# Attention with a memory and a two-layer MLP in one kernel: order of the first tokens' work, one product moved from GpSimd to VectorE, a third unit in float32, a second buffer for v

## The chip, the cores and the metric

The kernel runs on one core of one Trainium2 chip. The metric is the device time of one execution in microseconds (us), lower is better. Three runs of the kernel before gave 588.53, 588.90 and 590.05 us; their median is 588.9 us.

## The reference

Inputs are q, k and v of shape (4, 8, 576, 64), a memory `M_prev` of one 64x64 matrix per batch and head, a vector `z_prev` per batch and head, one `beta` per head, and two weight matrices: `w_in` (512x2048) and `w_out` (2048x512). With B = 4 batches, H = 8 heads, S = 576 tokens and D = 64:

```
local = softmax(causal(q k^T / 8)) v
q_p   = phi(q)                      (phi(x) = elu(x) + 1)
mem   = (q_p M_prev) / (q_p z_prev + 1e-6)
x     = g * mem + (1 - g) * local   (g = sigmoid(beta), per head)
out   = relu(x_tokens w_in)^2 w_out
```

`x_tokens` puts the eight heads of a token side by side (512 columns); there are 2304 tokens. Results are float32, and the kernel keeps nearly float32 exactness: most operands of TensorE are split into a high part in a faster format and the rest as a low part, and a product is then three products (high by high, low by high, high by low).

## The kernel before

**First tokens.** The first 64 tokens of each batch need only one 64x64 block of scores. `first_tokens` (L224 to L326) computes them for all batches and heads in two halves of two batches: loads, `scores(g)` on TensorE, `phi(g)` and `softmax(g)` on ScalarE, VectorE and GpSimd, `outputs(g)` with transposes, copies and products that end in `xh` (L318) and `xl` (L319), the split input of MLP block 0. The string `SEQ` (L55) gives the order in which the loads are issued on the SP queue: `a`, `b`, `c` are three parts of the first tokens' data of half 0 or 1, `g` the gates, `r` the raw data of one weight unit, `l` the loads of the first attention unit. The table `TE` (L65) says for five of their operations (`me`, `ze`, `se`, `xe`, `ye`, used at L272, L274, L279, L288, L294) whether VectorE (`d`) or GpSimd (`p`) does them, for half 0 and half 1.

**Weights.** The two matrices come in 32 units of 128 rows (512 KB each). `load_weight` (L170) issues the load, `split_weight` (L156) cuts a unit into a high and a low part with three VectorE operations (L162, L164, L168) and two ScalarE ones (L163, L167).

**Attention.** The remaining 512 tokens of each batch are worked off in 24 units of one batch, one pair of heads, and two or four tiles of 128 tokens. Units 0 to 3 are tiles 1 and 2 of batch 0, units 4 to 7 its tiles 3 and 4. Of units 0 to `NES` - 1 = 5 the scores are plain float32 products, of later ones three split products. Of units 0 and 1 (`NEF` = 2, `full`) also the product of the weights e with v is in float32: e is transposed on TensorE (L519), copied by ScalarE (L524) and multiplied with v as loaded (L563). From unit 2 on, v is scaled and split (L398 to L419), e is split into a 16-bit `a` (L542, L544), transposed by a DMA (L548) and multiplied in 16-bit pieces (L569 to L574), then summed (L576) into `s3`. `loads` (L332) issues the loads `kd`, `qm`, `vv` of the next unit on the SP queue as soon as the memory part of the current unit is in the program; `vv` has `VVB` = 1 buffer. A finished pair of tiles is stored to a scratch tensor `xd` (L595).

**MLP.** `moe(n)` (L695) takes 256 tokens: block 0 is the first tokens, blocks 1 to 6 follow, the last two blocks go together in `moe_pair`. The input of block n + 1 is read back from `xd` and transposed at step j = 6 of block n (`prefetch`, L609). A block has eight steps: 24 products `up` (L719 to L721), then on ScalarE the relu and square (L725, L726) and the rounded `gh` (L728; VectorE at L730 from block 4 on), on GpSimd `gl = r - gh` (L731), then 12 products `oacc` (L709 to L711), one step behind. `gh` has `GHB` = 3 buffers, `gl` `GLB` = 2, `r` one.

**Order.** All instructions of one engine run in a fixed order, in one queue per engine. A planner sets that order at compile time: it works off the program with estimated durations and gives every engine, among the instructions that are ready by its estimate, the one that comes first in the program. Hence attention, which stands ahead of the MLP blocks 1 to 8 in the program, goes first, and the MLP fills TensorE. The program mixes block 0, the weights and units 0 to 3 (`ORD`, L79). Instructions in a `tc.high_priority()` block come first whatever their place.

Of the kernel before, what the change touches and what calls it, by code (L numbers as in the profile page):

```python
# [8 lines left out]
F32 = mybir.dt.float32  # L9
# [5 lines left out]
ALU = mybir.AluOpType  # L15
AX = mybir.AxisListType

B, H, S, D = 4, 8, 576, 64
# [3 lines left out]
P = 128  # L22
# [4 lines left out]
QT = [(0, 64), (64, 128), (192, 128), (320, 128), (448, 128)]  # L27
NQ = len(QT)
SQ = S - D
GHB = 3  # L30
GLB = 2
PAIR = 0
SC = 16384.0
# [2 lines left out]
PM = 'pd'  # L36
FX = 'dd'
GHN = 4
VMIN = 2.0**-80
NEF = 2  # L40
NES = 6
PXT = 'up'
PXE = 'aa'
PHI = 1
QB = 2
VVB = 1
ZW = D + 1
MW = 576
WSC = 1.0 / 256.0
# [2 lines left out]
KB = 1  # L52
XB = 2
PJ = 6
SEQ = 'a0 b0 g a1 r b1 r c0 l r r c1'  # L55
W0 = 9
EARLY = 'dp'
LATE = 'dd'
# [3 lines left out]
SGROUP = {2: [[(2, 0, 320), (1, 0, 192)]], 1: [], 3: [[(3, 0, 448), (4, 0, 64)]], 4: [[(4, 64, 576)]]}  # L62
STG = [(9, 'hlx'), (8, 'hlx'), (3, 'hlx'), (0, 'hlx')]
XF = 0
TE = ['dd', 'dp', 'pp', 'pp', 'pp']  # L65
TC = 'aa'
TW = 2 * NP * 6 * D
GB = 2
# [21 lines left out]
def fused_kernel(ctx: ExitStack, tc: tile.TileContext, t0_d, zt_d, kk_d, qv_d, beta, w_in, w_out, out):  # L90
    nc = tc.nc
# [3 lines left out]
    at = ctx.enter_context(tc.tile_pool(name="at", bufs=1))  # L95
# [13 lines left out]
        out=mask, in_=mask, pattern=[[-1, MW]], compare_op=ALU.is_ge, fill=-1e30, base=448, channel_multiplier=1  # L109
# [114 lines left out]
    def first_tokens(tp, ahead):  # L224
# [4 lines left out]
        ng = B // GB  # L229
# [5 lines left out]
        for step in SEQ.split():  # L235
# [6 lines left out]
            else:  # L242
                g = int(step[1])
# [14 lines left out]
        def scores(g):  # L258
            sp[g] = sp0[:, g]
            qd = tr[g][:, : 2 * GD].rearrange("p (r i d) -> p i r d", r=2, i=GN)  # L260
            for i in range(GN):
                for h in range(2):
                    hd = slice(h * D, (h + 1) * D)
                    nc.tensor.matmul(sp[g][hd, i], qd[hd, i, 0], qd[hd, i, 1], start=True, stop=True)
# [54 lines left out]
            nc.vector.tensor_tensor(out=lo, in0=xb, in1=hi.bitcast(F32), op=ALU.subtract)  # L319

        sp0 = ps.tile([P, ng, GN, D], F32, tag="s", name="sp0")
        for g in range(ng):
            scores(g)
            phi(g)
        for g in range(ng):
            softmax(g)  # L326
            outputs(g)

    dp = ctx.enter_context(tc.tile_pool(name="dp", bufs=1, space=bass.MemoryType.DRAM))
    xd = [dp.tile([S, DM], F32, name=f"xd{b}") for b in range(B)]  # L330
# [14 lines left out]
    def attention(b, p, tiles, ld, after, early, sfull, full):  # L345
# [13 lines left out]
        if not sfull:  # L359
# [4 lines left out]
                out=ql[:, qa:qb], in0=q_raw[:, qa:qb], in1=qh[:, qa:qb].bitcast(F32), op=ALU.subtract  # L364
# [60 lines left out]
        for grp in (tiles[:2], tiles[2:]):  # L425
            ng = len(grp)
# [3 lines left out]
            for j, i in enumerate(grp):  # L430
# [13 lines left out]
                in0=pv[:, :, :, :D],  # L444
# [50 lines left out]
        for i in [t for t in TORD if t in tiles]:  # L495
            q0, n = QT[i]
# [60 lines left out]
            if full:  # L557
                s3 = acc[:, :, 0]
                for h in range(2):
                    hd = slice(h * D, (h + 1) * D)  # L560
                    for c in range(nb):
                        kp = D if c == 0 else P
                        nc.tensor.matmul(  # L563
                            acc[:n, h, 0], aT[:kp, h * nb + c, :n], v[:kp, c, hd], start=c == 0, stop=c == i
                        )
            else:
                for h in range(2):
                    o2 = acc[:n, h].rearrange("p j d -> p (j d)")
                    nc.tensor.matmul(o2, aT[:, h * nb, :n], vs[:, h, 0], start=True, stop=i == 0)  # L569
                    for c in range(1, i + 1):  # L570
                        nc.tensor.matmul(  # L571
                            acc[:n, h, 0], aT[:, h * nb + i + c, :n], vs[:, h, c, :D], start=False, stop=False
                        )
                        nc.tensor.matmul(o2, aT[:, h * nb + c, :n], vs[:, h, c], start=False, stop=c == i)  # L574
                s3 = at.tile([P, 2, D], F32, tag="s3", name="s3", bufs=2)
                nc.vector.reduce_sum(out=s3[:n], in_=acc[:n].rearrange("p h j d -> p h d j"), axis=AX.X)  # L576
            if FX[late] == "p" and not full:
                xo = memx[:n, i - 1].rearrange("p (h d) -> p h d", h=2)
# [116 lines left out]
    def moe(n):  # L695
        b, blk = blocks[n]
        xh, xl = xq.pop()
        pend = []
        acc = []

        def down(j, gh, gl):
            if j == 0:
                for t in range(2):
                    acc.append(ps.tile([P, DM], F32, tag="acc", name="oacc", bufs=2))
            last = j == NF // 2 - 1
            for u, t in [(u, t) for t in range(2) for u in range(2)] if last else [(u, t) for u in range(2) for t in range(2)]:
                f = 2 * j + u
                ts = slice(t * P, (t + 1) * P)
                nc.tensor.matmul(acc[t], gh[:, u, ts], w_out_op(f, 0), start=f == 0, stop=False)  # L709
                nc.tensor.matmul(acc[t], gh[:, u, ts], w_out_op(f, 1), start=False, stop=False)  # L710
                nc.tensor.matmul(acc[t], gl[:, u, ts], w_out_op(f, 0), start=False, stop=f == NF - 1)  # L711

        for j in range(NF // 2):
            need(1 + 8 * (j // 2 + 1))
            up = ps.tile([P, 2, BLK], F32, tag="up", name="up", bufs=2)
            for u in range(2):
                f = 2 * j + u
                for k in range(NK):
                    nc.tensor.matmul(up[:, u, :], w_in_op(f, k, 0), xh[:, k, :], start=k == 0, stop=False)  # L719
                    nc.tensor.matmul(up[:, u, :], w_in_op(f, k, 0), xl[:, k, :], start=False, stop=False)  # L720
                    nc.tensor.matmul(up[:, u, :], w_in_op(f, k, 1), xh[:, k, :], start=False, stop=k == NK - 1)  # L721
            r = mo.tile([P, 2, BLK], F32, tag="r", name="r", bufs=RB)
            gh = mo.tile([P, 2, BLK], F32R, tag="gh", name="gh", bufs=GHB)
            gl = mo.tile([P, 2, BLK], F32R, tag="gl", name="gl", bufs=GLB)
            nc.scalar.activation(r, up, AF.Relu, scale=WSC)  # L725
            nc.scalar.activation(r, r, AF.Square)  # L726
            if n < GHN:
                nc.scalar.copy(gh, r)  # L728
            else:
                nc.vector.tensor_copy(gh, r)  # L730
            nc.gpsimd.tensor_tensor(out=gl, in0=r, in1=gh.bitcast(F32), op=ALU.subtract)  # L731
            pend.append((j, gh, gl))
            yield
            if n == NBLK - 3 and j in (3, PJ):
                if j == 3:
                    xq.append(pair_tiles())
                pair_prefetch(xq[-1], int(j == PJ))
                yield
            elif j == PJ and n + 1 < NBLK:
                assert n > 0 or last  # L740
                xq.append(prefetch(*blocks[n + 1], *last))
                last.clear()
                yield
            if len(pend) > 1:
                down(*pend.pop(0))
                yield
        for x in pend:
            down(*x)
            yield
        for t in range(2):  # L750
            o = mo.tile([P, DM], F32, tag="x", name="o", bufs=XB)
            nc.scalar.activation(o, acc[t], AF.Copy, scale=WSC)
            if b is None:
                for u in range(2):
                    r0 = (2 * t + u) * S
                    nc.sync.dma_start(out[r0 : r0 + D, :], o[u * D : (u + 1) * D])
            else:
                r0 = b * S + QT[1 + 2 * blk + t][0]
                nc.sync.dma_start(out[r0 : r0 + P, :], o)
        yield  # L760
# [116 lines left out]
```

## Time and profile before

| | |
|---|---|
| median of three runs | 588.9 us |
| the profiled execution's own time | 588.17 us |
| its span, first to last instruction | 586.4 us |
| mean granted TensorE clock | 0.984 |
| busy: TensorE matmul | 546.1 us (93%) |
| busy: VectorE (DVE) | 386.1 us (66%) |
| busy: ScalarE (ACT) | 348.5 us (59%) |
| busy: GpSimd (POOL) | 122.6 us (21%) |

The span is what the trace shows; 1.8 us of the execution lie around it. TensorE's busy time counts matmuls to a modelled end, and consecutive matmuls overlap, so a full TensorE is read from the distance between starts, not from the duration of one. In the views below PE is TensorE, SPq the queue that issues the DMAs, and a row of a timeline has start, duration, engine, line, operation, result and operands, and in brackets the idle time of the engine before it with what ended it.

### The profile page before, as it was taken

How to read it: one execution, taken by the hardware profiler on the slowest of the kernel's cores; microseconds unless marked ns; L12 is line 12 of the kernel's file. 1: busy time of each engine (PE TensorE's matmuls, PEld its weight loads, DVE VectorE, ACT ScalarE, POOL GpSimd, SP SyncE). 2: the span in 40 equal slices, each digit the busy share in tenths (PEclk: the TensorE clock that was granted, in tenths of full speed). 3: DMA queues.
4: the chain of work that ended last, by engine and by line, in shares of the span. 5: the costliest groups of instructions: out<-in, count | busy, mean ns of one | idle time of the engine just before them, and what ended most of it. 6: DMA issues, size and time to landing. Idle time of an engine off the chain costs nothing.

```text
span 586.4 us, 11178 instructions
## 1 busy us (share of the span) xinstructions
PE 546.1 (93%) x4006; PEld 471.0 (80%) x4006; DVE 386.1 (66%) x1289; ACT 348.5 (59%) x791; POOL 122.6 (21%) x99
## 2 busy tenths in 40 slices
PE   2468999799999999999999999999999999999996
PEld 2347887588888888888888788888888898888885
DVE  5999989877878687997696687967887211000000
ACT  3789876578867587897566674676656222312222
POOL 2502131124322011121120201111011212122221
PEclk9987999899999999999999999999999999999999
DMA  8967673757645667795553547555253300000001
GB/s 290 409 197 280 222 193 92 165 131 187 133 120 118 152 154 167 147 200 152 126 141 109 125 111 163 116 148 147 69 118 81 108 19 1 36 1 0 2 0 72
DMA packets 127574, 76.24 MB, mean 130 GB/s; under 512 B 99360, under 2 KB 112672, under 8 KB 127520
## 3 DMA queue, kind: packets, MB, share of 16 engines
q1 hardware_dynamic: 127520, 75.55, 48.8%
q8 instruction: 31, 0.51, 0.4%
q14 instruction: 23, 0.19, 0.1%
HBM read 42.63 MB, written 8.78 MB: 88 GB/s over the span
## 4 chain that ended last, share of the span: by engine, by line
PE 64%; DVE 17%; DMA 10%; issue 4%; ACT 3%; SPq 1%; POOL 1%; ACTq 0%; DVEq 0%; POOLq 0%
PE oacc L711 6%; PE oacc L709 6%; PE up L721 6%; PE up L719 6%; PE up L720 6%; PE oacc L710 6%; PE sp L465 5%; DMA aT<-a 4%; DVE w L168 3%; PE up L670 2%; PE up L669 2%; PE up L668 2%; PE acc L574 2%; DMA vv<-in_qv_dram 2%; PE pm L433 2%
## 5 line engine op out<-in xcount | busy, mean ns | idle before, releaser
L731 POOL TENSOR_TENSOR gl<-r,gh 128x512 fp32r<-128x512 f32 x56 | 77.3, 1380 | 332.4 <-ACT gh L728 118.1
L719 PE MATMUL up<-xh,w 128*128 128x256 f32 x448 | 130.1, 290 | 4.1 <-ACT aF L524 4.1
L720 PE MATMUL up<-xl,w 128*128 128x256 f32 x448 | 130.1, 291 | 0.0
L721 PE MATMUL up<-xh,w 128*128 128x256 f32 x448 | 130.0, 290 | 0.0
L504 ACT ACTIVATE e<-e,mx 128x320 f32<-128x320 f32 (+3 forms) x128 | 77.8, 610 | 83.1 <-DVE memx L584 43.0
L719 PEld LDWEIGHTS up<-xh,w 128*128 128x128 f32 x448 | 87.3, 195 | 8.0 <-ACT aF L524 4.5
L709 PE MATMUL oacc<-w,gh 128*128 128x512 f32 x224 | 90.1, 402 | 0.6 <-DVE gh L730 0.6
L720 PEld LDWEIGHTS up<-xl,w 128*128 128x128 f32 x448 | 87.4, 195 | 2.5 <-issue 0.8
L721 PEld LDWEIGHTS up<-xh,w 128*128 128x128 f32 x448 | 87.3, 195 | 2.3 <-issue 1.5
L710 PE MATMUL oacc<-w,gh 128*128 128x512 f32 x224 | 88.7, 396 | 0.0
L711 PE MATMUL oacc<-w,gl 128*128 128x512 f32 x224 | 86.8, 398 | 0.5 <-POOL gl L731 0.4
L544 DVE SCALAR_TENSOR_TENSOR a<-e,a 128x128 f16<-128x128 f32 x120 | 67.8, 583 | 28.2 <-ACT a L542 27.5
L542 ACT ACTIVATE a<-e 128x128 f16<-128x128 f32 x120 | 56.1, 519 | 8.8 <-DMA aT<-a 6.7
L676 DVE CAST gh<-r 128x512 fp32r<-128x512 f32 x16 | 6.9, 428 | 79.3 <-ACT r L675 79.3
L711 PEld LDWEIGHTS oacc<-w,gl 128*128 128x128 f32 x224 | 41.5, 188 | 10.3 <-POOL gl L731 1.8
L484 DVE CUSTOM_DVE_ANT_0 e<-sp,mask 128x320 f32<-128x320 f32 (+3 forms) x128 | 47.8, 418 | 1.4 <-PE sp L465 1.2
L725 ACT ACTIVATE r<-up 128x512 f32<-128x512 f32 x56 | 32.7, 583 | 26.5 <-PE up L721 23.2
L709 PEld LDWEIGHTS oacc<-w,gh 128*128 128x128 f32 x224 | 42.3, 189 | 7.5 <-DVE gh L730 0.8
L710 PEld LDWEIGHTS oacc<-w,gh 128*128 128x128 f32 x224 | 42.3, 189 | 7.4 <-issue 0.7
L674 ACT ACTIVATE r<-up 128x512 f32<-128x512 f32 x16 | 9.6, 599 | 61.8 <-PE up L670 61.8
L574 PE MATMUL acc<-vs,aT 128*128 128x128 f16 x308 | 36.7, 220 | 0.0
L571 PE MATMUL acc<-vs,aT 128*128 128x64 f16 x308 | 35.5, 193 | 0.0
(154 smaller groups left out, 1132.8 us busy)
## 6 DMA issues: line engine op xcount, KB each, us to landing
raw<-in_w_in_dram SPq DMA_DIRECT2D x11, 512.0 KB, 6.7
vv<-in_qv_dram SPq DMA_DIRECT2D x16, 320.0 KB, 3.2
raw<-in_w_out_dram SPq DMA_DIRECT2D x9, 512.0 KB, 7.1
kd<-in_kk_dram SPq DMA_DIRECT2D x16, 288.0 KB, 3.2
out_dram<-o SPq DMA_DIRECT2D x16, 256.0 KB, 2.2
xd<-memx SPq DMA_DIRECT2D x31, 128.0 KB, 2.1
xn<-xd SPq DMA_DIRECT2D x14, 256.0 KB, 2.9
qm<-in_qv_dram SPq DMA_DIRECT2D x8, 321.0 KB, 3.4
```

Source lines behind the costliest of these rows:

```text
L484: nc.vector.tensor_tensor_reduce(out=e[:, h, ka:kb], in0=sps[:, h, cs], in1=mask[:, 448 - q0 + ka : 448 - q0 + kb], scale=-0.125, scalar=3 ...
L504: ex = nc.scalar.activation(e[:n, h, :ke], e[:n, h, :ke], AF.Exp, bias=bs, scale=-1.0, accum_out=sm[:n, h : h + 1])
L542: nc.scalar.mul(av[:, :, o0 : o0 + w], x, SC)
L544: nc.vector.scalar_tensor_tensor(out=av[:, :, o0 + w : o0 + 2 * w], in0=x, scalar=SC, in1=av[:, :, o0 : o0 + w], op0=ALU.mult, op1=ALU.sub ...
L574: nc.tensor.matmul(o2, aT[:, h * nb + c, :n], vs[:, h, c], start=False, stop=c == i)
L709: nc.tensor.matmul(acc[t], gh[:, u, ts], w_out_op(f, 0), start=f == 0, stop=False)
L710: nc.tensor.matmul(acc[t], gh[:, u, ts], w_out_op(f, 1), start=False, stop=False)
L711: nc.tensor.matmul(acc[t], gl[:, u, ts], w_out_op(f, 0), start=False, stop=f == NF - 1)
L719: nc.tensor.matmul(up[:, u, :], w_in_op(f, k, 0), xh[:, k, :], start=k == 0, stop=False)
L720: nc.tensor.matmul(up[:, u, :], w_in_op(f, k, 0), xl[:, k, :], start=False, stop=False)
L721: nc.tensor.matmul(up[:, u, :], w_in_op(f, k, 1), xh[:, k, :], start=False, stop=k == NK - 1)
L731: nc.gpsimd.tensor_tensor(out=gl, in0=r, in1=gh.bitcast(F32), op=ALU.subtract)
```

## The change

It does six things. (1) `SEQ`: all loads of the first tokens come ahead of the first weight unit, and five weight units instead of four are loaded there, four of them behind the loads of the first attention unit. (2) The whole arithmetic of the first tokens stands in `tc.high_priority()`. (3) `TE`: seven products of the first tokens go from GpSimd to VectorE. (4) `GLV`: `gl` of MLP blocks 0 to 6 (56 instructions) is computed by VectorE; the last pair stays on GpSimd. (5) `NEF`: unit 2 too is done in float32 with v as loaded. (6) `vv` gets a second buffer; `gh` goes from three to two and `s3` from two to one.

```
-GHB = 3
+GHB = 2
+GLV = range(7)
-NEF = 2
+NEF = 3
-VVB = 1
+VVB = 2
-SEQ = 'a0 b0 g a1 r b1 r c0 l r r c1'
+SEQ = 'a0 b0 g a1 b1 c0 c1 r l r r r r'
-TE = ['dd', 'dp', 'pp', 'pp', 'pp']
+TE = ['dd', 'dd', 'dd', 'dd', 'dd']
...
-        for g in range(ng):
-            scores(g)
-            phi(g)
-        for g in range(ng):
-            softmax(g)
-            outputs(g)
+        with tc.high_priority():
+            for g in range(ng):
+                scores(g)
+                phi(g)
+            for g in range(ng):
+                softmax(g)
+                outputs(g)
...
-                s3 = at.tile([P, 2, D], F32, tag="s3", name="s3", bufs=2)
+                s3 = at.tile([P, 2, D], F32, tag="s3", name="s3", bufs=1)
...
-            nc.gpsimd.tensor_tensor(out=gl, in0=r, in1=gh.bitcast(F32), op=ALU.subtract)
+            (nc.vector if n in GLV else nc.gpsimd).tensor_tensor(out=gl, in0=r, in1=gh.bitcast(F32), op=ALU.subtract)
```

## Rows read from the trace of the kernel before

**Rows 1.** Busy time by stretch: start:end length, each engine (instructions), granted clock, DMA, GB/s.
```profile
0.00:15.00 15.00, 3.94 (x64) 3.57 (x64) 9.02 (x28) 5.07 (x8) 4.64 (x10) 1.00 0.90 293
15.00:30.00 15.00, 7.18 (x52) 5.43 (x52) 15.00 (x40) 10.54 (x23) 7.39 (x7) 1.00 1.00 398
...
45.00:60.00 15.00, 12.96 (x75) 11.81 (x75) 15.00 (x38) 14.38 (x35) 3.62 (x2) 0.77 0.64 245
60.00:90.00 30.00, 29.02 (x189) 25.48 (x188) 27.91 (x77) 25.08 (x63) 7.37 (x6) 1.00 0.69 203
90.00:120.00 30.00, 25.19 (x185) 19.91 (x186) 24.49 (x88) 16.13 (x34) 4.65 (x5) 0.94 0.55 133
120.00:450.00 330.00, 326.22 (x2682) 285.33 (x2682) 263.56 (x943) 228.62 (x537) 63.04 (x47) 1.00 0.57 134
```

**Rows 2.** Timeline of TensorE at the start of the MLP and around 110 us.
```profile
43.23 3.23 PE L563 MATMUL acc<-vv,aF 64*128 64x64 f32 x12
...
46.22 0.56 PE L720 MATMUL up<-xl,w 128*128 128x256 f32 x1
...
108.87 0.48 PE L621 MATMUL px<-identr,memx 128*128 128x128 f32 x2
112.59 1.32 PE L465 MATMUL sp<-kd,qm 64*128 64x512 f32 x4 [3.24 <-DVE mx L484]
```

**Rows 3.** Instructions on tile xh up to 120 us: shortest/median/longest ns, first and last start.
```profile
L319 DVE TENSOR_TENSOR xl<-xp,xh x2: 655/667/679, 33.6 to 41.7; 128x512 fp32r<-128x512 f32 x2
```

**Rows 4.** VectorE by line and shape, 0 to 130 us: count, busy us, mean ns, idle before.
```profile
L168 DVE TENSOR_TENSOR w<-hw,w 128x512 fp32r<-128x512 f32 x8 | 6.8, 856 | 0.0
...
L576 DVE TENSOR_REDUCE s<-acc 128x128 f32<-128x256 f32 x6 | 2.2, 415 | 0.0
...
L544 DVE SCALAR_TENSOR_TENSOR a<-e,a 128x512 f16<-128x512 f32 x2 | 1.4, 680 | 0.0
...
L274 DVE TENSOR_TENSOR tr<-tr,w 128x512 f32<-128x512 f32 x1 | 0.7, 672 | 0.0
```

**Rows 5.** Timeline of all engines around 25 us.
```profile
24.89 0.15 DVE L549 SCALAR_TENSOR_TENSOR sm<-sm,gpm 128x2 f32<-128x2 f32 x1
...
25.11 1.16 POOL L294 TENSOR_TENSOR w<-w,t 128x512 f32<-128x512 f32 x1 [1.44 <-DVE sm L549]
25.30 1.00 DVE L549 SCALAR_TENSOR_TENSOR sm<-sm,gpm 128x2 f32<-128x2 f32 x1
```

**Rows 6.** The chain of waits between 60 and 120 us: start, length, what.
```profile
82.95 4.90 DMA hw<-in_w_out_dram
...
101.34 3.60 DMA vv<-in_qv_dram
```

**Rows 7.** Waits over the whole span: who waited for whom, total us, times, longest.
```profile
POOL gl L731 <- ACT gh L728: 118.1, 19, 10.0
...
DVE vx L398 <- DMA vv<-in_qv_dram: 17.3, 11, 3.3
```

**Rows 8.** Waits of the SP queue over the whole span, same columns.
```profile
SPq L342 <- DVE vs L415: 49.6, 18, 7.4
```

**Rows 9.** Timeline of TensorE from the last product of a step to the next.
```profile
64.45 0.39 PE L711 MATMUL oacc<-w,gl 128*128 128x512 f32 x1
64.68 0.28 PE L719 MATMUL up<-xh,w 128*128 128x256 f32 x1
64.79 0.28 PE L720 MATMUL up<-xl,w 128*128 128x256 f32 x1
```

**Rows 10.** Instructions on tile gl, whole span: shortest/median/longest ns, first and last start.
```profile
L731 POOL TENSOR_TENSOR gl<-r,gh x56: 1262/1294/2040, 57.1 to 492.1; 128x512 fp32r<-128x512 f32 x56
```

**Rows 11.** Timelines of SP, VectorE and TensorE at the border to MLP block 5.
```profile
356.67 0.38 SPq L595 DMA_DIRECT2D xd<-memx  x1
...
373.91 0.68 DVE L625 TENSOR_TENSOR xl<-px,xh 128x512 fp32r<-128x512 f32 x1
...
376.06 0.39 PE L719 MATMUL up<-xh,w 128*128 128x256 f32 x1
```

## The prediction

> **What bounds the kernel now.** I read busy time by stretch first [rows 1]. From 120 to 450 us TensorE is busy 326.2 of 330 us, so a change there helps only if it keeps TensorE full. Up to 60 us it is the other way round: VectorE is busy 15.0 of 15 us from 15 us on, while TensorE has 7.2 of 15 us and then 13.0 of 15 at a granted clock of 0.77, a mixture of its levels 2.4 and 1.2 GHz. From 90 to 120 us neither is full (25.2 and 24.5 of 30). The time to win lies ahead of 120 us.
>
> The timeline of TensorE says what it lacked. MLP block 0 needs `xl` of both halves; the second `xl` starts at 41.7 us and takes 0.67 [rows 3], and the second kind of product starts at 46.2, behind 3.2 us of attention [rows 2]. At 108.9 us the last input of block 1 (unit 3's tiles) is transposed, and then TensorE stands for 3.2 us behind a score's maximum [rows 2]. In the chain of waits between, VectorE's work alternates with DMAs that came late: 4.9 us for a weight unit at 83 us, 3.6 us for `vv` at 101 us [rows 6]. SP is one reason: its `vv` load waited 49.6 us in all for the previous unit to finish with v, up to 7.4 us each, with all later loads behind it [rows 8].
>
> **The change, part by part. First tokens.** Seven products go from GpSimd to VectorE. The same product on VectorE took 0.67 us [rows 4]: 7 x 0.67 = 4.7 us more on the engine that is full there. Against that, VectorE no longer stands behind them: a two-column L549 took 0.15 us alone and 1.00 us when a GpSimd product had started just before, and it ended with it [rows 5]. L168 on `hw`, of the same shape as L274, averages 0.86 against 0.67 [rows 4], 8 x 0.19 = 1.5 us. I take 5 us back up to 120 us (bounds: the 0.85 + 1.5 = 2.4 shown, and the 9 us that seven products of 1.3 us would hold it if each blocked it throughout; 1.3 from [rows 10]). With priority and their loads first, `xl` comes sooner: VectorE was idle 6 of the first 15 us [rows 1], so its work starts near 6 us; each half has about ten full-width operations of 0.67 us and 1.6 us of small ones, 16.6 us for both, and 1.4 us of gates, so it ends near 24 us; transposes, copies and products behind it add about 4. So `xl` is complete near 28 us instead of 42.4, by some 14 us. The price is that the weights load later: 3 MB of first tokens at the 398 GB/s of [rows 1] take 7.5 us, and with the loads moved ahead of it I put the first weight some 3 us later than now (an estimate: 1.2 MB of the 3 MB are new ahead of it). That is hidden by the first tokens' 16.6 us on VectorE, without which it would cost those 3 us.
>
> **Unit 2 in float32** takes off VectorE four L544 of at most 0.68 us and two L576 of 0.42 [rows 4], at least 2.5 us with its smaller forms, and the scaling of v; I take 3. Two DMA transposes leave the SP queue. TensorE gets 20 more products and 10 transposes; 12 such products took 3.2 us at the low clock [rows 2], 0.27 each, so up to 8 us, in a stretch where it has 8 us of 15 free at first (if that cover is gone, the 8 us are lost).
>
> **`gl` on VectorE.** On GpSimd one takes 1.29 us [rows 10], on VectorE I price it as L274: 0.67 us. Its 56 are spread evenly from 57.1 to 492.1 us [rows 10]; seven fall before 120 us: +4.7 us. So VectorE's account up to 120 us is +4.7 - 5 - 3 + 4.7 = +1.4 us: nearly nothing. Between 120 and 450 us there are about 41: +27.5 us; GpSimd gone from beside it gives back 0.2 us each, 8 us (between zero and the 0.85 of [rows 5], nearer zero since most operations aren't hit). VectorE goes from 263.6 to 283 of 330 us, 80% to 86% [rows 1]. New is also where it waits: GpSimd stood 118 us for `gh` with nothing behind it [rows 7]; on VectorE the attention's operations stand behind a `gl` that waits. The chain itself gets 0.6 us shorter per step.
>
> **Buffers.** The second `vv` ends the SP waits of [rows 8] and VectorE's 17.3 us for `vv` [rows 7], most of which TensorE didn't feel; ahead of 110 us I take 3 us (bounds 0 and the 4.9 + 3.6 of [rows 6]). `gh` with two buffers costs nothing as long as `gl`, which has two already and the same reader, suffices: GpSimd was last held by `gh` being made, not by a full buffer [rows 7]; without that cover it would be up to the 0.67 us of one `gl` a step. `s3` is written and read by VectorE alone: nothing.
>
> **The sum.** Block 0 gets a lead of up to 14 us, but block 1 can't start before unit 3 is done (108.9 us), and that hangs on VectorE, whose account is even. What is won there is what block 0 still had to do after it: 24 products `up` at 0.11 us and 12 `oacc` at 0.23, start to start [rows 9], 2.7 + 2.8 = 5.5 us, with about 1.2 us of the low clock. The gate itself moves by the 3 us of late loads less 1.4, 1.6. That is 8.3 us. Later, each block waits for its attention, and at block 5 there is little air: the store at 356.7, `xl` done at 374.6, its first product at 376.1 [rows 11]. A TensorE that runs 8 us ahead finds attention not quite as far ahead: I give back 2 us. 588.2 - 8.3 + 2 = 581.9; the median stands 0.7 us over the profiled execution, so 582 us with the rounding down.
>
> On the shared port, the Trainium skill (SBUF — State Buffer, Who interferes with whom) says that a VectorE operation with two SBUF inputs and a GpSimd operation that reads SBUF exclude each other for the whole instruction of whichever began first. The trace agrees in the one case of [rows 5]. By that rule taken to its end, each `gl` moved could free up to its full 1.29 us and VectorE's account after 120 us would be even: the 2 us given back would stay, 580.
>
> **The rivals.** *The whole lead stays* (0.24): block 0's 14 us carry over because attention, relieved of the SP waits, moves up as far as the MLP. For it speak the 49.6 us of [rows 8]; against it VectorE's full 15 of 15 us, which the change does not empty. 588.2 - 14 - 1.2 = 573.
>
> *The load order moves only who waits* (0.13): the first tokens come early, the weights later, the gate at 108.9 stays or moves back by the 1.4 us of VectorE's account, and the planner's new order leaves another idle stretch like the 3.2 us of [rows 2]. The change would not do what it says, for TensorE would be fed no sooner in sum: 588.
>
> *VectorE becomes the bound between 120 and 450 us* (0.18). Every `gl` then delays attention by its 0.67 less 0.2 us, and by what it waits for `gh` in VectorE's queue. Up to block 5 there are some 29: 14 us, of which the margin of 1.5 us [rows 11] covers little, and TensorE stands; it decides once attention falls back by more than that margin and the 6 us gained. 588.2 - 6.3 + 14 - 1.5 = 594.4, say 595. For it speaks that attention ends just in time at block 5; against it that VectorE would have 14% left and TensorE other work at most times. [...]
>
> **How the numbers follow.** Forecast 0.45 (577 to 587), whole lead 0.24, no net change 0.13, VectorE bound 0.18. A measurement of this kernel can tell about 0.3%, 1.8 us, from no change. Faster than that: 0.45 + 0.24 and a quarter of the third case, 0.72; same: the rest of it, 0.10; slower: 0.18. The range reaches from 571, below the whole lead, to 595, the slow rival; outside lie its tail and planner's orders not seen here.
>
> **What would show it.** First tokens: `xl` of both halves done by 30 us, first `up` products with `xl` before 36; if `xl` is early and `up` isn't, the weights were the limit. VectorE's two-column L549 at 0.15 us throughout, `gl` near 0.67. The gate: unit 3's L621 at 105 to 109 us, no `up` of block 0 behind it. The SP row L342 <- L415 gone. VectorE at 85% to 88% between 120 and 450 us with TensorE's idle time there still under 5 us; if TensorE has 10 us or more there and attention's stores come just ahead of the blocks, the third rival holds. The forecast is wrong if block 1 starts as now, or if TensorE is full from 110 us on and the span still doesn't fall.

## The result, and the profile after

The changed kernel takes 582.8 us (median of 4 runs, 581.8 to 583.95) against 589.28 us before (4 runs, 588.53 to 590.05): a ratio of 0.9881, 95% interval 0.9857 to 0.9906, 6.5 us or 1.2% faster. The profiled span falls from 586.4 to 581.7 us. The forecast of 582.0 us and its sign held; the first step of its reasoning did not. Here and below, ratios and their intervals leave out executions more than 1.5% above the fastest of their kernel and medians do not; without them the median is 588.39 us in place of 589.18 for the changed kernel with two float32 units, and 595.15 in place of 595.41 for the second v buffer alone.

Busy time by stretch of the changed kernel, same columns as [rows 1]:

```profile
0.00:15.00 15.00, 3.94 (x64) 3.57 (x64) 7.93 (x26) 3.05 (x5) 1.82 (x8) 1.00 0.88 288
15.00:30.00 15.00, 2.08 (x8) 1.27 (x8) 15.00 (x45) 11.83 (x25) 1.73 (x1) 1.00 0.88 347
45.00:60.00 15.00, 14.65 (x98) 13.15 (x98) 14.32 (x42) 14.25 (x37) 1.22 (x1) 0.89 0.83 318
60.00:90.00 30.00, 29.89 (x199) 25.80 (x198) 28.27 (x88) 27.36 (x72) 4.23 (x2) 1.00 0.60 182
90.00:120.00 30.00, 29.25 (x219) 24.01 (x218) 28.98 (x95) 21.85 (x45) 3.30 (x2) 1.00 0.62 164
120.00:450.00 330.00, 326.03 (x2673) 285.13 (x2672) 277.74 (x966) 226.15 (x529) 5.57 (x5) 1.00 0.58 134
```

From 15 to 30 us TensorE does less than before (2.1 against 7.2 us), and from 60 to 120 us more: 59.1 against 54.2 us. From 120 us on it is as full as it was (326.0 against 326.2 us), although VectorE now has 277.7 us there in place of 263.6. So the time was won between 30 and 120 us, and TensorE's timeline shows how:

```profile
30.91 1.94 PE L304 MATMUL px<-identr,w 128*128 128x128 f32 x8 [12.73 <-ACT w L168]
...
36.44 1.09 PE L304 MATMUL px<-identr,w 128*128 128x128 f32 x8
...
43.46 0.39 PE L721 MATMUL up<-xh,w 128*128 128x256 f32 x1 [0.74 <-ACT xh L319]
...
46.09 0.41 PE L722 MATMUL up<-xl,w 128*128 128x256 f32 x1 [0.34 <-DVE xl L320]
...
49.29 0.41 PE L722 MATMUL up<-xl,w 128*128 128x256 f32 x1
...
49.85 0.28 PE L722 MATMUL up<-xl,w 128*128 128x256 f32 x1
...
108.19 0.40 PE L623 MATMUL px<-identr,memx 128*128 128x128 f32 x2
...
109.42 1.13 PE L467 MATMUL sp<-kd,qm 64*128 64x512 f32 x4
...
114.28 0.36 PE L721 MATMUL up<-xh,w 128*128 128x256 f32 x1
```

The first tokens come later, not sooner: TensorE waits 12.7 us for their transposes, and the first product with `xl` starts at 46.09 us, where it was 46.22 [rows 2]. But from then on TensorE hardly stops: from 60 to 120 us it is idle for 0.9 us, where it was 5.8. The 3.24 us stop behind the last transposes for block 1 [rows 2] is gone (the score at 109.42 follows at once), and block 1 begins at 114.3 us where it began at 118.1. The granted clock is the lower one from 46.3 to 49.7 us and doesn't come back before the end; before, it was the lower one from 38.3 to 48.5, from 55.4 to 58.8 and from 113.4 to 116.8 us.

The start of the clock column is not to be read as it stands. The record of the granted clock begins at 36.1 us in this trace and at 31.5 us in the one before; ahead of that the column shows 1.00 for want of a record, in the first rows of [rows 1] too. TensorE was at 1.2 GHz there: the same eight transposes take 1.94 us at 30.91 and 1.09 at 36.44 (above), and in the kernel before sixteen products of one kind change at 31.5 us:

```profile
29.04 1.12 PE L314 MATMUL xp<-wx,tr 128*64 128x64 f32 x16
...
31.61 0.69 PE L314 MATMUL xp<-wx,tr 128*64 128x64 f32 x16 [0.41 <-ACT wx L305]
```

**An account that adds up.** I cut each trace into steps of 1 us with the view of busy time by stretch. What TensorE's busy time leaves of a step is idle; its busy time times one less the granted clock is lost to the clock; the rest is work at full speed. Ahead of the first record of the clock I count the lower clock. The three sum to the span, by their definition. Some matmul records are missing from each trace, so a term is good to 1 or 2 us; and each account is of the one execution that was profiled, whose time lies up to 1.7 us from the median.

| kernel | span | idle | clock loss | work | block 1 starts |
|---|---|---|---|---|---|
| before | 586.4 | 40.4 | 13.4 | 532.6 | 118.1 |
| after | 581.7 | 36.7 | 7.3 | 537.7 | 114.3 |

Of the clock loss, 6.2 us before and 5.6 us after lie ahead of the first record. The third float32 unit adds work (the six kernels here with two such units have 531 to 534 us of it, the eight with three 534 to 542, the 542 in the one with repeated transposes). The change pays 5.1 us of work and saves 3.7 us of idle time and 6.1 us of clock loss: 4.7 us. Later blocks keep about what block 1 won: block 4 starts 1.6 us sooner than before, block 5 4.5 (371.6 against 376.1 [rows 11]), the end 4.7.

**GpSimd beside VectorE.** The operations named in [rows 5, 10], after the change:

```profile
L551 DVE SCALAR_TENSOR_TENSOR sm<-sm,vz x58: 124/153/163, 94.7 to 445.5; 128x2 f32<-128x2 f32 x58
L551 DVE SCALAR_TENSOR_TENSOR sm<-sm,gpm x6: 103/149/153, 26.0 to 69.0; 128x2 f32<-128x2 f32 x6
...
L733 DVE TENSOR_TENSOR gl<-r,gh x56: 657/684/1339, 58.0 to 487.4; 128x512 fp32r<-128x512 f32 x56
```

No L551 takes longer than 0.163 us now, where one took 1.00 [rows 5], and `gl` takes 0.68 us where GpSimd took 1.29 [rows 10]. Over the whole trace I compared each VectorE operation that overlaps a GpSimd one with the median of its line and shape without: some 21 us lost before, 3.6 us after; 9.2 and 1.6 us of that up to 120 us.

### The profile page after: what moved, and what is told of

Same layout as the page of the kernel before. It is cut to its first block, busy times and chain, and to the rows that moved or that the text cites. A ratio compares the mean times of both kernels' runs of the same rounds, so it can differ in the third digit from the quotient of the medians.

```text
span 581.7 us, 11097 instructions
## 1 busy us (share of the span) xinstructions
PE 544.9 (94%) x4019; PEld 469.7 (81%) x4019; DVE 406.3 (70%) x1338; ACT 349.3 (60%) x794; POOL 39.4 (7%) x36
## 4 chain that ended last, share of the span: by engine, by line
PE 62%; DVE 22%; DMA 9%; ACT 4%; issue 2%; SPq 1%; ACTq 0%; DVEq 0%
PE oacc L713 6%; PE oacc L711 6%; PE oacc L712 6%; PE up L723 6%; PE up L722 6%; PE up L721 6%; PE sp L467 4%; DVE e L486 3%; PE up L672 2%; PE up L671 2%; PE up L670 2%; DVE a L546 2%; DMA aT<-a 2%; DVE w L169 2%; PE pm L435 2%
## 5 line engine op out<-in xcount | busy, mean ns | idle before, releaser
L722 PE MATMUL up<-xl,w 128*128 128x256 f32 x448 | 128.3, 286 | 0.3 <-DVE xl L320 0.3
L721 PEld LDWEIGHTS up<-xh,w 128*128 128x128 f32 x448 | 86.3, 193 | 5.0 <-ACT xh L319 1.0
L722 PEld LDWEIGHTS up<-xl,w 128*128 128x128 f32 x448 | 86.2, 192 | 3.0 <-issue 0.6
L723 PEld LDWEIGHTS up<-xh,w 128*128 128x128 f32 x448 | 86.2, 192 | 1.3 <-issue 0.7
L713 PE MATMUL oacc<-w,gl 128*128 128x512 f32 x224 | 85.4, 398 | 0.8 <-DVE gl L733 0.8
L546 DVE SCALAR_TENSOR_TENSOR a<-e,a 128x128 f16<-128x128 f32 x116 | 66.0, 577 | 24.1 <-ACT a L544 23.6
L713 PEld LDWEIGHTS oacc<-w,gl 128*128 128x128 f32 x224 | 40.9, 188 | 9.3 <-DVE gl L733 1.9
L679 POOL TENSOR_TENSOR gl<-r,gh 128x512 fp32r<-128x512 f32 x16 | 20.7, 1292 | 379.9 <-DVE gh L678 379.9
L733 DVE TENSOR_TENSOR gl<-r,gh 128x512 fp32r<-128x512 f32 x56 | 39.1, 699 | 2.9 <-ACT gh L730 1.7
```

The source lines that it names most:

```text
L546: nc.vector.scalar_tensor_tensor(out=av[:, :, o0 + w : o0 + 2 * w], in0=x, scalar=SC, in1=av[:, :, o0 : o0 + w], op0=ALU.mult, op1=ALU.sub ...
L733: (nc.vector if n in GLV else nc.gpsimd).tensor_tensor(out=gl, in0=r, in1=gh.bitcast(F32), op=ALU.subtract)
```

## The experiments

Twelve kernels, measured in four groups; each group has its own runs of the kernel before (medians 589.46, 589.57, 590.44 and 589.76 us), and ratios are to those.

**One part undone.** Each takes one part out of the changed kernel.

*Products back on GpSimd:*
```diff
-GLV = range(7)
+GLV = range(0)
```


> The changed kernel with gl of blocks 0 to 6 back on GpSimd, all else as changed. Theory A (the gain is made up to 120 us by unit 2 in float32 and the second buffer of v; gl on VectorE is about even, since what it adds is given back by operations that no longer stand behind GpSimd): 583 us, 581 to 585, VectorE between 120 and 450 us back near 264 us from 278. Theory B (the gain is that GpSimd is out of VectorE's way): at least 3 us lost, 586 us or more. Theory C (gl on VectorE costs and hides part of the gain): 580 us or less.

Measured 593.93 us, ratio 1.0078 (1.0048 to 1.0107): slower than the kernel before, 11 us above the changed one. VectorE by line and shape between 120 and 450 us (count, busy us, mean ns, idle before) in the changed kernel:

```profile
L586 DVE SCALAR_TENSOR_TENSOR memx<-s,sm,memx 128x64 f32<-128x64 f32 x102 | 24.3, 279 | 0.9
...
L551 DVE SCALAR_TENSOR_TENSOR sm<-sm,vz 128x2 f32<-128x2 f32 x52 | 5.9, 151 | 0.2
...
L384 DVE SCALAR_TENSOR_TENSOR qm<-pe,qm 128x256 f32<-128x256 f32 x9 | 3.8, 420 | 1.6 <-ACT qm L383 1.6
```

And the same three in this one:

```profile
L586 DVE SCALAR_TENSOR_TENSOR memx<-s,sm,memx 128x64 f32<-128x64 f32 x106 | 31.8, 341 | 1.2
...
L551 DVE SCALAR_TENSOR_TENSOR sm<-sm,vz 128x2 f32<-128x2 f32 x54 | 10.4, 233 | 0.3
...
L384 DVE SCALAR_TENSOR_TENSOR qm<-pe,qm 128x256 f32<-128x256 f32 x9 | 6.6, 736 | 2.2 <-ACT qm L383 2.1
```

Its busy time by stretch:

```profile
120.00:450.00 330.00, 320.90 (x2645) 281.51 (x2645) 276.84 (x935) 223.22 (x523) 61.70 (x47) 0.99 0.60 136
```

42 `gl` of 0.70 us, 29.6 us, are gone from VectorE in that stretch, and it is as busy as with them: 276.8 against 277.7 us. The same operations take longer beside GpSimd; the loss over the whole trace comes to 31 us, where the changed kernel has 3.6. Not every kind of operation pays: 64 SCALAR_TENSOR_TENSOR beside GpSimd lost 23.7 us, 22 TENSOR_REDUCE and 9 RECIPROCAL nothing. And TensorE has 5 us less there. The expectation of 583 us is refuted, and that of 586 us or more (GpSimd out of VectorE's way) holds; on this order the offload saves VectorE nothing.

*One buffer for v:*
```diff
-VVB = 2
+VVB = 1
```


> The changed kernel with one buffer for v. Theory A: the loads on SP wait again for v, TensorE between 60 and 120 us falls from 59.1 us busy towards 57, 585 to 586 us. Theories B and D (D: the first tokens' order makes the gain): no change, 582 to 584 us.

Measured 592.59 us, 1.0062 (1.0041 to 1.0083), some 7 us more than expected. The SP queue's waits (who waited for whom, total us, times, longest), of the changed kernel:

```profile
SPq L344 <- DVE vs L417: 25.5, 15, 3.7
```

And of this one:

```profile
SPq L344 <- DVE vs L417: 42.9, 17, 6.9
```

With two buffers the wait of [rows 8] is halved, not gone; with one it is nearly what it was. TensorE's idle time between 30 and 60 us is 7.4 us here and 3.4 in the changed kernel; most of the rest is idle time after 120 us (6.7 against 4.0) and clock loss (9.4 against 7.3). Between 60 and 120 us, where the expectation looked for the loss, TensorE is as busy as in the changed kernel (59.0 us).

*Two float32 units:*
```diff
-NEF = 3
+NEF = 2
```


> The changed kernel with units 0 and 1 alone in float32 with v. Theory A: unit 2 gets its v scaling and its DMA transposes back, unit 2's store moves from 84 us towards 97 us, 585 to 587 us. Theories B and D: 582 to 584 us.

Measured 589.18 us, 0.9981 (0.9957 to 1.0005). Busy time by stretch:

```profile
60.00:90.00 30.00, 27.68 (x190) 23.56 (x189) 28.32 (x86) 23.55 (x55) 1.76 (x2) 1.00 0.70 197
90.00:120.00 30.00, 25.33 (x162) 19.68 (x164) 24.52 (x84) 20.55 (x47) 3.30 (x2) 0.89 0.53 143
```

Without the third float32 unit TensorE stands between 60 and 120 us again (53.0 us busy in place of 59.1), as in the kernel before, and the clock falls there. The time is above the 585 to 587 us expected.

*First tokens as before* (old `SEQ`, old `TE`, no priority):
```diff
-SEQ = 'a0 b0 g a1 b1 c0 c1 r l r r r r'
+SEQ = 'a0 b0 g a1 r b1 r c0 l r r c1'
...
-TE = ['dd', 'dd', 'dd', 'dd', 'dd']
+TE = ['dd', 'dp', 'pp', 'pp', 'pp']
...
-        with tc.high_priority():
+        if True:
```


> The changed kernel with the first tokens as before: load order, engines and no priority. Theory A: the first tokens' part wins nothing (their last split ended later with it, at 46.0 us against 42.4), so 582 to 584 us. Theory D: the gain is theirs, 587 to 590 us.

Measured 587.22 us, 0.9963 (0.9946 to 0.9980). The second `xl` starts at 40.1 us, 5 us sooner than in the changed kernel, and the kernel is 4.4 us slower, as by theory D: its idle time is the same (36.9 us), its clock loss 14.0 us in place of 7.3.

**One part alone**, in the kernel before, in the order of the four expectations (the last is the reverse of the diff above, with the priority):

```diff
-NEF = 2
+NEF = 3
...
-            nc.gpsimd.tensor_tensor(out=gl, in0=r, in1=gh.bitcast(F32), op=ALU.subtract)
+            nc.vector.tensor_tensor(out=gl, in0=r, in1=gh.bitcast(F32), op=ALU.subtract)
...
-VVB = 1
+VVB = 2
...
-GHB = 3
+GHB = 2
...
-                s3 = at.tile([P, 2, D], F32, tag="s3", name="s3", bufs=2)
+                s3 = at.tile([P, 2, D], F32, tag="s3", name="s3", bufs=1)
...
-SEQ = 'a0 b0 g a1 r b1 r c0 l r r c1'
+SEQ = 'a0 b0 g a1 b1 c0 c1 r l r r r r'
```

> The kernel before with the third float32 unit alone. Theory P (each part does its own work, as the prediction summed it): 3 us less VectorE work ahead of 110 us, so 585 to 588 us, and TensorE busy at least 2 us more between 60 and 120 us than the 54.2 us of before. Theory E (the parts need each other: this one takes work from VectorE only where VectorE is what TensorE waits for): 588 to 591 us, TensorE between 60 and 120 us within 1 us of before. Theory N (what counts is only that the planner's order came out anew, and it moves the time by some us either way): a time with no tie to the window that the part touches, the blocks after 120 us at another pace than in the kernel before by more than 2 us.

> The kernel before with the products of blocks 0 to 6 on VectorE alone. Theory P: between 120 and 450 us TensorE stays at 326 us busy and VectorE comes to 277 to 283 us, the first-token products stay on GpSimd, so 587 to 590 us. Theory C (GpSimd beside VectorE costs as much as the products, and taking it away is the change's main gain, as the undo of this part at 593.9 us suggests): 578 to 584 us. Theory N: any time between 583 and 595 us with the pace after 120 us off by more than 2 us either way.

> The kernel before with the second buffer for v (and the two buffers given up for it) alone. Theory P: the 18 us wait of the load of v at 50 us is gone and TensorE is busy 2 to 4 us more between 30 and 120 us: 585 to 587 us. By the undo (592.6 against 582.8 us) the part would be worth 10 us: 578 to 581 us. Theory E (worth it only where the first tokens and the products leave VectorE room): 587 to 590 us. Theory N: slower than 590 us or faster than 583 us with the gain or loss after 120 us.

> The kernel before with the part on the first tokens alone: order of loads, seven operations from GpSimd to VectorE, priority. Theory P without the lead (the last xl at 44 to 47 us as in the changed kernel): 3 to 5 us more VectorE work ahead of 40 us and nothing won, 588 to 592 us. Theory P with the lead (xl done by 30 us): 574 to 580 us. By the undo (587.2 against 582.8 us) it would be worth 4.4 us: 584 to 586 us. Theory N: a time outside these, from blocks after 120 us.

| part | alone: us, ratio (interval) | undone: us | idle and clock loss, alone | undone |
|---|---|---|---|---|
| third float32 unit | 588.28, 0.9986 (0.9968 to 1.0004) | 589.18 | 37.0 + 12.5 | 42.7 + 8.8 |
| `gl` on VectorE | 589.93, 1.0006 (0.9979 to 1.0034) | 593.93 | 37.0 + 19.1 | 44.2 + 10.2 |
| second `vv` | 595.41, 1.0077 (1.0051 to 1.0103) | 592.59 | 44.5 + 16.6 | 43.1 + 9.4 |
| first tokens | 585.93, 0.9933 (0.9910 to 0.9956) | 587.22 | 41.7 + 12.2 | 36.9 + 14.0 |

In the table's order, the undoings (each less 582.8) make the parts worth 6.4, 11.1, 9.8 and 4.4 us, 31.7 together; alone (each against 589.57) they give 1.3 us, a loss of 0.4, a loss of 5.8 and 3.6 us, less than nothing together; all four give 6.5. So the parts' worths don't add. Against the expectations: the third unit lies where the times of theories P and E meet, with TensorE 58.3 us busy between 60 and 120 us, as P had it; `gl` lies within P (587 to 590), the second `vv` outside all but N, and the first tokens where their undoing put them (584 to 586), with the last `xl` at 45.5 us, no lead. `gl` alone added 9.4 us to VectorE between 120 and 450 us (273.0 us busy, under the 277 to 283 expected), left TensorE at 326.0 and won nothing, since the clock loss rose by 5.7 us while the idle time fell by 3.4.

**How much is the planner's order?** The same edit of buffers without the second `vv`:

```diff
-GHB = 3
+GHB = 2
...
-                s3 = at.tile([P, 2, D], F32, tag="s3", name="s3", bufs=2)
+                s3 = at.tile([P, 2, D], F32, tag="s3", name="s3", bufs=1)
```


> The kernel before with the two buffers given up (two for gh in place of three, one for s3 in place of two) and one buffer for v as before. Theory P (they cost nothing): 588.5 to 591 us, and then the 595.4 us of the second v buffer alone is that buffer's own doing. Theory B (the buffers given up are what cost those 6 us): 594 to 597 us with the blocks from 300 us on late, as there. Theory N: any other time, 584 to 588 or above 597 us.

Measured 586.82 us, 0.9946 (0.9921 to 0.9971), theory N: 3.6 us faster by taking two buffers away. On a fixed order that could hardly do anything but add waits, so I put the gain down to the order that the planner wrote anew: a matching of VectorE's sequence of operations (by operation, tiles and shape) with that of the kernel before finds 63% of it. With the second `vv` on top, which on a fixed order takes a wait away, it is 595.4 us; by the two ratios that is some 8 us more. Every edit of this study but the next one leaves only 42% to 67% of VectorE's order in the kernel that it edits, and by these two runs such a rewriting may move the time by 3 us and more either way; that it was the order, and not the buffers in some other way, is argued, not shown. So no part's price here is free of it.

The same question, with an edit that does nothing:

```diff
-    nc.vector.tensor_copy(mask0[D:], mask[D:, 512 : 512 + D])
+    nc.vector.tensor_copy(mask0[D:], mask[D:, 512 : 512 + D]); junk = cp.tile([P, D], F32, name="junk"); nc.vector.tensor_copy(junk[:D], mask[:D, 448 : 448 + D])
```


> The changed kernel with one more 64x64 copy on VectorE at the start (0.2 us of work that nobody reads), which makes the planner write its order anew. Theory P (the parts' own work decides): 581.5 to 584.5 us, as the changed kernel. Theory N (any new order moves the time by some us, and the changed kernel's 582.8 us is partly a lucky one): 585 to 594 us, with TensorE's windows off by 2 us or more both ahead of 120 us and after it. Theory E (the parts support each other): 581.5 to 585 us, since all parts are there.

Measured 582.93 us, 0.9877 (0.9846 to 0.9908). It was meant to force a new order, and didn't: the sequences on VectorE and ScalarE came out the same as in the changed kernel, place by place. So it says nothing on orders. What it does say: the same order, built again and run on another occasion, gives the same time (582.8 and 582.9 us).

**Does an early `xl` pay?** The weights' first operations on VectorE and ScalarE are held behind the first tokens:

```diff
-            nc.vector.tensor_scalar(out=u0, in0=u0, scalar1=29, scalar2=None, op0=ALU.logical_shift_right)
-            nc.scalar.activation(f1, f1, AF.Prelu, scale=2.0**-111, alpha=-(2.0**32))
+            v = nc.vector.tensor_scalar(out=u0, in0=u0, scalar1=29, scalar2=None, op0=ALU.logical_shift_right)
+            a = nc.scalar.activation(f1, f1, AF.Prelu, scale=2.0**-111, alpha=-(2.0**32))
...
+            tc.add_manual_dep(v.ins, lead['v'].ins.name, AFTER, reason='weights come behind')
+            tc.add_manual_dep(a.ins, lead['a'].ins.name, AFTER, reason='weights come behind')
```
(`lead`, set elsewhere in the edit, holds the last L295 product and the last copy to `wx`.)

> The changed kernel with the weights' first VectorE operation held behind the last first-token product and their first ScalarE operation behind the last first-token copy, so that the lead that the prediction counted on comes about. All expect the last xl done by 34 us instead of 46.0. Theory L (an early xl is worth its lead less what the gate takes back, as the prediction had it): 576 to 581 us, first up step before 40 us. Theory W (the first up waits for the split weights as much as for xl, and VectorE has the same work ahead of 115 us either way): first up at 42 to 47 us, 582 to 587 us. Theory N: 585 to 594 us with the loss after 120 us.

Measured 590.37 us, 1.0001 (0.9969 to 1.0033), a time that only theory N allowed, though the loss came ahead of 120 us and not after. The first `xl` starts at 28.9 us and the second at 39.1 (not by 34), the first `up` at 37.6, 6 us ahead of the changed kernel; block 1 begins at 125.8, 11.5 us behind it. Busy time by stretch between 30 and 60 us and TensorE's timeline there and ahead of block 1:

```profile
30.00:60.00 30.00, 23.18 (x136) 19.16 (x131) 27.20 (x72) 26.47 (x64) 2.13 (x2) 0.72 0.53 188
```
```profile
34.50 0.63 PE L523 MATMUL pxa<-identr,e 128*64 128x128 f32 x4 [1.55 <-ACT aF L528]
37.57 0.58 PE L723 MATMUL up<-xh,w 128*128 128x256 f32 x1 [2.45 <-ACT w L170]
...
42.23 0.41 PE L725 MATMUL up<-xh,w 128*128 128x256 f32 x1
42.45 0.41 PE L723 MATMUL up<-xh,w 128*128 128x256 f32 x1
...
49.17 0.28 PE L724 MATMUL up<-xl,w 128*128 128x256 f32 x1
49.29 0.28 PE L725 MATMUL up<-xh,w 128*128 128x256 f32 x1
...
52.56 0.44 PE L523 MATMUL pxa<-identr,e 128*128 128x128 f32 x2 [2.55 <-DMA qm<-in_qv_dram]
...
56.35 0.41 PE L723 MATMUL up<-xh,w 128*128 128x256 f32 x1
...
116.03 0.45 PE L623 MATMUL px<-identr,xn 128*128 128x128 f32 x3 [3.56 <-DMA xn<-xd]
...
119.64 0.43 PE L625 MATMUL px<-identr,memx 128*128 128x128 f32 x1
```

TensorE stands 2.45 us for the weights; then its steps come 0.21 us apart (42.23, 42.45), at 1.2 GHz, and 0.12 apart (49.17, 49.29) at 2.4 GHz. It stands 2.55 us again, and the clock is down again. Against the changed kernel: idle time 37.7 us (+1.0), clock loss 16.6 us (+9.3). The idle time is 6.9 us less up to 30 us and 7.9 us more behind, so the lead went into later stops and into the low clock, in about equal parts. One of the later stops is the 3.56 us for the input of block 1, which is read back at 113.6 and 115.8 us (100.2 and 103.8 in the changed kernel); its last transpose comes at 119.64 instead of 108.3 us, which accounts for the delay of block 1. What held the read-back up was not taken apart. In the twelve timed runs of this one program, whose order is fixed, time and mean granted clock go together: 587.9 us at 0.985 at one end, 594.4 us at 0.971 at the other.

**Is it the clock?** The same kernel with TensorE kept at work in both stops, by doing two batches of transposes again:

```diff
+FILL = {3: 5, 4: 6}
...
-                    for x in range(bn):
+                    tag5.append(0)
+                    for x in list(range(bn)) * FILL.get(len(tag5), 1):
```


> The kernel with the weights held behind the first tokens (590.4 us), with two batches of TensorE's transposes done again (five times the batch that ends at 35.1 us, six times the one that ends at 50.0 us there), so that TensorE works through most of its two idle times of 2.45 and 2.55 us ahead of the stretches at the lower clock; the results are the same. Theory C (the early start lost its lead to the clock, which fell to 1.2 GHz when TensorE, just started, stood still): granted clock above 0.9 between 30 and 60 us where it was 0.72, the up steps behind the first one 0.12 us apart and not 0.215, block 1 begun by 121 us where it was 125.8, 583 to 587 us. Theory R (the lead is lost for other reasons, VectorE and the weights): the clock may rise but the time goes into waits, or the clock falls all the same: block 1 at 125 us or later, 589 to 592 us. Theory N (new order, new time): order of TensorE nearly the one before, so a time outside both would need another cause.

Measured 588.14 us, 0.9968 (0.9946 to 0.9990): by the medians 2.2 us faster than without the repetition, though TensorE does more. That is at the edge of the noise, since the intervals of the two ratios overlap. Busy time by stretch and TensorE's timeline:

```profile
30.00:60.00 30.00, 23.31 (x140) 18.76 (x139) 28.05 (x75) 26.52 (x65) 2.15 (x2) 0.89 0.56 202
```
```profile
32.79 2.37 PE L525 MATMUL pxa<-identr,e 128*64 128x128 f32 x20 [1.51 <-ACT aF L530]
35.91 0.39 PE L725 MATMUL up<-xh,w 128*128 128x256 f32 x1 [0.74 <-ACT w L171]
...
39.15 0.48 PE L727 MATMUL up<-xh,w 128*128 128x256 f32 x1 [0.79 <-DVE w L172]
...
40.13 0.42 PE L725 MATMUL up<-xh,w 128*128 128x256 f32 x1
...
42.93 0.28 PE L725 MATMUL up<-xh,w 128*128 128x256 f32 x1
...
46.66 3.37 PE L525 MATMUL pxa<-identr,e 128*64 128x128 f32 x26
53.54 0.79 PE L715 MATMUL oacc<-w,gh 128*128 128x512 f32 x1 [3.51 <-ACT gh L734]
```

The first low stretch shrinks from 10.2 us (35.8 to 46.1) to 3.4 (39.3 to 42.7). The second stop moved: TensorE, further ahead, now waits 3.5 us for `gh`, and the clock falls with it again, for 3.4 us in place of 6.8. In the account of the two profiled executions, which lie 4.4 us apart, the clock loss falls by 7.6 us (16.6 to 9.0) and idle time by 3.2, the repeated and other work adds 6.4. Theory C just missed its marks (granted clock 0.89 for 0.9, block 1 at 122.0 us for 121, 588.1 us for 587), and theory R missed its own (125 us, 589). So work put into the stops cut the low stretches here, and the low clock was a part of what the lead had lost; how much of the time that bought stays open, since the edit left only 67% of VectorE's order and 60% of TensorE's. Neither kernel beats the changed one, which stays the fastest of all.

## Why the prediction was right or wrong

The number and the sign were right; the account behind them only in part. That the total came out 0.8 us from the forecast is luck to a good part: the terms that were to make the 6.3 us gave 3.8 us at block 1 where 8.3 were summed, most of them from a source that the sum had priced at 1.2 us, and 4.7 us at the end of the profiled executions.

- **"`xl` is complete near 28 us instead of 42.4": wrong, the step that failed.** It was complete at 46.0 us. The sum had counted VectorE's 16.6 us of first-token work as uninterrupted, and it isn't; and it took 4 us for what stands behind that work, where it was 13.7. VectorE's timeline in the changed kernel:

```profile
25.51 0.19 DVE L293 RECIPROCAL t<-t 128x8 f32<-128x8 f32 x1
25.62 0.37 DVE L163 TENSOR_SCALAR raw<-raw 128x512 uint32<-128x512 uint32 x1
...
30.09 0.67 DVE L295 TENSOR_TENSOR w<-w,t 128x512 f32<-128x512 f32 x1
30.68 0.68 DVE L169 TENSOR_TENSOR w<-raw,w 128x512 fp32r<-128x512 f32 x1
...
45.36 0.68 DVE L320 TENSOR_TENSOR xl<-xp,xh 128x512 fp32r<-128x512 f32 x1
```

  Between 6 and 40 us VectorE does some 17 us for the first tokens, 18 us for weights and 3 us for attention (durations, which overlap a little), mixed in the planner's order, priority or not. Its last first-token product (L295) ends at 32.3 us, not near 24; behind it, copies and transposes stand among weights on ScalarE and VectorE once more. And an `xl` at 28.9 and 39.1 us, made by force, was worth nothing (590.4 us); a lead as long as the forecast one was never made.
- **The gate.** Right in place: the transposes for block 1 at 108.19 us, inside the 105 to 109 named. Wrong in what stood behind it: products of block 0 were still left until 113.6 us, so block 1 came 3.8 us sooner, not 8.3. The gate itself moved by 0.7 us, not 1.6. These 3.8 us came from the 3.24 us stop that is gone and from the clock, of which the sum had only 1.2 us, where 6.1 us were saved, less the third unit's extra work. An early block 1 is not the gain by itself: it begins at 113.2 us with the two buffers given up alone and at 114.4 us with the third unit alone, and the spans of these fall by 3.4 and 1.6 us, not by 4.7.
- **"Minus 2 given back at block borders": not in the end.** The lead shrank to 1.6 us at block 4 and grew again to 4.5 at block 5, where block 5 in the kernel before had waited for its `xl` [rows 11].
- **Contention with GpSimd: right.** 5 us up to 120 us and 8 us behind were taken; some 7.7 and 9.6 us are gone. Taken to its end, as the prediction did with each `gl` freeing its full 1.29 us, it would have been 41 x 1.29 = 53 us behind 120 us, far more than the even account that it drew from it; 9.6 came.
- **`gl` on VectorE: right in price, a little high in sum.** 42 of 0.70 us between 120 and 450 us where about 41 of 0.67 were counted. VectorE 84% busy (277.7 us) for 283 forecast and 85% to 88% given as the sign, TensorE idle 4.0 us there. The third rival, VectorE as the bound, didn't come; the run with `gl` on GpSimd shows the reverse, TensorE losing 5 us with the offload. The Trainium skill (Perfetto Trace Analysis, Optimizing Scalar/DVE Operations) allows such an offload from a saturated VectorE, but warns that between these two engines it might not help, since they share a read port of SBUF; the 276.8 against 277.7 us agree with the warning. The rule on the shared port in the Trainium skill (SBUF — State Buffer, Who interferes with whom) agrees with the 31 us lost beside GpSimd in that run.
- **Unit 2 in float32: mis-sized.** 3 us less VectorE work was taken; its total is 0.7 us smaller with the unit than without (406.3 and 407.0 us), 0.9 alone (385.2 and 386.1). Yet undoing it cost 6.4 us. In the profiled execution, 4.0 us longer than the changed kernel's, TensorE has 7.5 us more of stops and low clock and 3.5 us less work, and between 60 and 120 us alone it is idle 6.1 us longer.
- **Buffers.** "Ends the SP waits": halved, 49.6 to 25.5 us. VectorE's wait for `vv` fell from 17.3 to 5.5 us. "Costs nothing" of the buffers given up: alone they even gained 3.6 us, which no step foresaw. The 3 us that the second `vv` was to bring ahead of 110 us were not found: alone, it lost time.
- **The whole lead stays (573)** and **the load order moves only who waits (588)**: neither came. The second comes nearest for the first-token part, whose `xl` came no sooner, but the rest of the change won time without it.

Still open: how much of the 6.5 us belongs to the change and how much to the order that came out with it. Taking two buffers away moved the time by 3.6 us, as I argue through the order, so a share of that size can't be excluded. Nor can it be excluded that the parts need one another, which would also make them worth more undone than alone; the run that was to part the two left the order as it was. That the order the planner wrote for the changed kernel leaves TensorE few stops between 46 and 125 us is shown; that the four parts had to lead to it is not.

## What to carry to other kernels

Where a planner writes the order, test a part both ways, undone and alone, and keep an account of idle time, clock loss and work for each: when the two ways disagree, as here by 31.7 us against a loss of 1.3, no part has a price of its own, and the order is a suspect. Starting an engine sooner was worth nothing where it then stopped: ask for the first moment from which it can run through. Check a clock column against the same products at both ends of it before counting with it. Before moving work to GpSimd to spare VectorE, compare the means of VectorE's operations beside it and alone.

## What the runs showed of the hardware

In each of the 14 traces TensorE's early transposes ran at 1.2 GHz (214 ns from start to start; the same ones 109.5 ns at 2.4 GHz in the changed kernel) up to a moment between 25.6 and 40.9 us, and the record of the granted clock begins only there.

With stops of TensorE of 2.45 and 2.55 us, after work at 2.4 GHz, went 10.2 and 6.8 us at 1.2 GHz, which cost 4.2 and 3.3 us of clock loss, more than the stops themselves; in the kernel before, the stop of 3.24 us at 109 us [rows 2] was followed by 3.4 us, which cost 1.7. The length of a stop doesn't settle it: in the changed kernel the clock fell at 46.3 us with no stop longer than 1.27 us since 31 us. Between 30 and 60 us the clock of the kernel before shows two such stretches:

```profile
30.00:60.00 30.00, 22.83 (x152) 19.13 (x148) 30.00 (x79) 27.99 (x68) 4.58 (x3) 0.77 0.64 229
```

It had not been expected either that VectorE would be as busy without 42 operations as with them while another engine did them at the same time. Of the other operations' 28.7 us more between 120 and 450 us, 24.8 us are the excess of those that overlapped one of GpSimd.
